# Earlier loads in the fourth chunk, inverse roots on GpSimd and a new order of steps in an adaLN / long convolution / token-MLP kernel

## The chip, the cores and the metric

One core of a Trainium2 chip runs the kernel. The metric is the device time of one execution in microseconds, the median over the runs shown. All tensors are float32. Matrix products run on TensorE (PE in the profile), elementwise work on VectorE (DVE), ScalarE (ACT) and GpSimd (POOL); all DMAs of the part around the change are issued by SyncE (SP).

## What is computed

2048 tokens (S), 640 channels (D), a token MLP of width 1728 (F):

```python
mod = (_silu(c) @ w_mod).reshape(c.shape[0], 6, 1, -1)
sa, ca, ga, sb, cb, gb = (mod[:, 0], ..., mod[:, 5])
h = _layernorm(x, axis=-1) * (1 + ca) + sa                 # x = A_q
x = x + ga * _A_ref(h, A_k, A_v, A_shift_k, A_ssm_k, A_ssm_D)
h = _layernorm(x, axis=-1) * (1 + cb) + sb
x = x + gb * _B_ref(h, B_w1, B_b1, B_w2, B_b2)
```

`_A_ref` is a short causal convolution of k over 4 tokens, times v, then a causal convolution over all 2048 tokens for each channel (by Fourier transform), times h. `_B_ref` is a layer norm of its own, then a product with w1 over the token axis, a tanh GELU, and a product with w2 back to tokens.

## The kernel before

**Chunks.** The channels are worked on in five chunks of 128 (`c` from 0 to 4; "the fourth chunk" is `c == 3`). For each chunk the Fourier transform is done as matmuls with constant matrices: `step1` (line 230) is the first stage, `f2` (line 249) the second, in eight groups `g`, each with its product of the two spectra on VectorE (L60, into `p`) and a sum on GpSimd (into `y`); `i2` (line 280) and `i1` (line 302) are the two inverse stages. `gate` multiplies the result by the layer-normed input, `add_x` adds it to the residual rows `XR(j)`, and `spill` writes these to DRAM. While one chunk goes through its inverse stages, `step1` of the next chunk runs in between.

**Loads for the tail of the program.** In the fourth chunk thirteen loads are kept in a list, `later`: nine pieces of 128 x 640 of `w_mod` (`one`, into the tiles `in`, `t` and `rows`) and four pieces of `w1` (`some`, into `aux`). `next_load()` takes the next of them: ScalarE writes one column of the place (line 543), which makes it wait until the place is free, and SyncE's DMA (line 601 or 606) waits for that write. So the position of `next_load()` in ScalarE's order paces the load. Beside them SyncE copies rows of `w1` into a scratch tensor `wc` (`copy_rows`).

**The last chunk and the start of the MLP.** With `c == 4` the loop is left after `i2`, and what follows is written out by hand. The tokens lie in 16 row blocks (`j`). For each of them the last chunk's gate must be applied, then the second layer norm: `stats` (bn_stats and bn_aggr on VectorE), `root_in` (variance to standard deviation, ScalarE), `root` (its reciprocal, corrected by one Newton step, VectorE, `newton`), `norm1` (ScalarE), `times` and `plus` (scale and shift by the modulation, VectorE; `mean` in between corrects a sum on ScalarE). The factor of h in w1's product is again normed: `square` (ScalarE) gives the variance of the scaled rows, a second root follows, then `half` (ScalarE, writes the high part of the operand) and `rest` (VectorE, the low part). All float32 operands of the MLP are split into a high and a low part, and a product is three matmul pairs: high x high, high x low, low x high (`mm`, line 465). `products` does those of the first four blocks of 128 of F, `blk[0]` to `blk[3]`, for a pair of row blocks; the weights' parts are written by `split_rows` and `split_third` (high on ScalarE, L442 and L435; low on VectorE, L60).

**What sets the order.** Each engine works through its instructions in program order; semaphores tie them. The order of this part is a list of words, which a loop runs through: `st 2 3` calls `stats(2)` and `stats(3)`, and so on (`q` root_in, `R` root, `n` norm1, `t` times, `m` mean, `p` plus, `s` square, `h` half, `r` rest, `Q` products of a pair, `v`/`wl` low parts and `vh`/`wh` high parts of the weights, `gr`/`gm`/`ga` gate and add of the rest, `gb` one row of the modulation). The table `roots` says which variances a root handles together: before, root n takes the second variances of one pair of row blocks and the first ones of the pair behind it:

```python
roots = (((), (0, 1)), ((0, 1), (2, 3)), ((2, 3), (4, 5)), ((4, 5), (6, 7)), ((6, 7), (8, 9, 10, 11)),
         ((8, 9), (12, 13)), ((10, 11), (14, 15)), ((12, 13), ()), ((14, 15), ()))
```

`warm(t, n)` (line 853) issues n matmuls whose result nobody reads, between the last inverse stages and ahead of the first products.

## Time and profile before

| | |
|---|---|
| median of 3 runs | 668.79 us (664.34 to 676.61) |
| the profiled execution's own time | 667.48 us |
| its span, first to last instruction | 665.6 us, 20814 instructions |
| mean granted TensorE clock | 0.984 |
| busy share of ACT, DVE, POOL | 47%, 75%, 21% |
| HBM read, written | 79.63 MB, 19.14 MB |

The profile is one execution. A row of a timeline has start and duration in us, engine, line of the kernel, operation, out<-in, and in brackets the idle time ahead of it with what ended it. A row of the chain of waits has start, duration and what the program's end waited for in that time; "issue" there is time in which the engine waited for nothing that the profile shows. PE is the matmul itself, PEld the load of its weights, SPq the issue of a DMA by SyncE. "PEclk" is the clock that TensorE was granted, 1.00 being full speed.

### The profile page before, as it was taken

Reading aid. Unit: us, or ns where it says so; the run is one execution under the profiler, and the core shown is the slowest. Engines: PE = TensorE matmul, PEld = TensorE weight load, DVE = VectorE, ACT = ScalarE, POOL = GpSimd, SP = SyncE. Lnnn points to the kernel's source line nnn. Section 1 sums busy time; section 2 is a strip of 40 time slices with the busy share of each in tenths; the row PEclk is TensorE's granted clock in tenths of the full one; section 3 lists DMA queues with packets and bytes.
Section 4 is the critical chain, followed back from the end, with each engine's and each line's share of the span. In section 5 each row is a group of like instructions: output and inputs, shape, how many; then the busy total and the mean of one; then the engine's idle time right before and its main releaser. Section 6 shows DMA issues by size and latency. Waiting matters only on the chain.

```text
span 665.6 us, 20814 instructions
## 1 busy us (share of the span) xinstructions
PE 618.9 (93%) x9089; PEld 597.4 (90%) x9089; DVE 497.0 (75%) x844; ACT 311.0 (47%) x497; POOL 138.3 (21%) x138
## 2 busy tenths in 40 slices
PE   0599878899999989999999999999999999999997
PEld 0699458799999979799999999999999999999997
DVE  7788559988888847789974214756688888888886
ACT  0574365555736637667874304343342332333331
POOL 5284017684865027000000000000000000000000
PEclk9999679999999989999999999999999999999999
DMA  9967997818642645514008530975698555345601
GB/s 183 215 200 209 383 177 154 187 41 193 129 77 67 196 125 154 182 33 96 1 1 156 97 64 1 218 210 145 191 354 264 173 180 159 101 143 170 189 32 39
DMA packets 175568, 98.01 MB, mean 147 GB/s; under 512 B 89939, under 2 KB 165494, under 8 KB 175222
## 3 DMA queue, kind: packets, MB, share of 16 engines
q1 hardware_dynamic: 170930, 95.38, 54.4%
q10 hardware_dynamic: 4548, 1.31, 1.1%
q8 instruction: 71, 1.16, 0.7%
q14 instruction: 19, 0.16, 0.1%
HBM read 79.63 MB, written 19.14 MB: 148 GB/s over the span
## 4 chain that ended last, share of the span: by engine, by line
PE 82%; DVE 9%; DMA 3%; issue 2%; ACT 2%; SPq 1%; ACTq 0%; DVEq 0%
PE pst L1173 26%; PE pst L465 23%; PE pst L230 11%; PE pst L249 9%; PE pst L280 5%; PE pst L1038 4%; PE pst L302 2%; DVE tap L60 2%; DMA aux<-in_w_mod_dram 2%; DVE kt L60 1%; DVE p L60 1%; DVE aux L60 1%; PE tap L366 1%; PE pst L377 1%; DMA in<-in_A_v_dram 1%
## 5 line engine op out<-in xcount | busy, mean ns | idle before, releaser
L249 PEld LDWEIGHTS pst<-z,w 128*64 128x64 f32 x2560 | 76.0, 138 | 9.0 <-issue 5.7
L249 PE MATMUL pst<-z,w 128*64 128x64 f32 x2560 | 77.5, 222 | 6.9 <-DVE p L60 4.4
L230 PE MATMUL pst<-v,x 128*64 128x128 f32 x640 | 45.1, 299 | 23.9 <-DVE x L60 23.3
L230 PEld LDWEIGHTS pst<-v,x 128*64 128x64 f32 x640 | 43.0, 221 | 24.6 <-issue 24.1
L235 ACT ACTIVATE z<-pst 128x1024 f32<-128x1024 f32 (+2 forms) x45 | 41.4, 932 | 46.0 <-PE pst L230 25.6
L60 DVE TENSOR_TENSOR p<-pst,kt 128x512 f32<-128x512 f32 x80 | 51.0, 683 | 14.7 <-ACT kt L255 13.3
L60 POOL TENSOR_TENSOR y<-p 128x256 f32<-128x256 f32 x72 | 54.2, 776 | 35.1 <-DVE p L60 34.7
L280 PEld LDWEIGHTS pst<-v,y 32*128 32x128 f32 x1280 | 39.0, 192 | 3.0 <-issue 1.6
L280 PE MATMUL pst<-v,y 32*128 32x64 f32 x1280 | 40.5, 277 | 0.6 <-ACT z L235 0.6
L230 PE MATMUL pst<-v,p 128*64 128x128 f32 x640 | 38.8, 280 | 1.9 <-issue 1.8
L230 PEld LDWEIGHTS pst<-v,p 128*64 128x64 f32 x640 | 36.5, 140 | 2.7 <-issue 2.2
L255 ACT ACTIVATE kt<-pst 128x512 f32<-128x512 f32 x40 | 24.0, 599 | 31.1 <-PE pst L249 13.0
L1173 PE MATMUL pst<-r_z,m_w 128*128 128x320 f32 x198 | 37.2, 309 | 0.0
L60 POOL TENSOR_TENSOR t<-in,t 128x512 f32<-128x512 f32 x20 | 30.3, 1524 | 18.1 <-DMA in<-in_A_k_dram 17.1
L60 DVE TENSOR_TENSOR tap<-tap,kt 128x512 f32<-128x512 f32 x45 | 31.4, 697 | 1.3
L60 DVE TENSOR_TENSOR kt<-in,tap 128x512 f32<-128x512 f32 x45 | 30.8, 685 | 1.4
L1173 PEld LDWEIGHTS pst<-r_z,m_w 128*128 128x128 f32 x198 | 31.1, 188 | 0.0
L288 ACT ACTIVATE z<-pst 128x512 f32<-128x512 f32 x38 | 21.6, 664 | 18.7 <-PE pst L280 18.7
L1110 ACT ACTIVATE m_w<-m_v 128x896 fp32r<-128x896 f32 x19 | 17.9, 948 | 26.3 <-DVE m_v L60 14.7
L302 PEld LDWEIGHTS pst<-z,v 64*64 64x64 f32 x1280 | 22.2, 144 | 7.9 <-issue 4.3
L302 PE MATMUL pst<-z,v 64*64 64x64 f32 x1280 | 24.1, 229 | 4.0 <-issue 2.9
L60 DVE TENSOR_TENSOR aux<-aux,g 128x1024 f32<-128x1024 f32 (+1 forms) x14 | 26.3, 1885 | 0.2
(309 smaller groups left out, 1446.6 us busy)
## 6 DMA issues: line engine op xcount, KB each, us to landing
x<-in_B_w_dram SPq DMA_DIRECT2D x18, 512.0 KB
m_v<-in_B_w_dram SPq DMA_DIRECT2D x20, 384.0 KB
aux<-in_A_ssm_k_dram SPq DMA_DIRECT2D x10, 512.0 KB
out_dram<-m_w SPq DMA_DIRECT2D x32, 160.0 KB
in<-in_A_k_dram SPq DMA_DIRECT2D x36, 128.0 KB
in<-in_A_v_dram SPq DMA_DIRECT2D x36, 128.0 KB
ts<-m_p SPq DMA_DIRECT2D x10, 320.0 KB
m_w<-xs SPq DMA_DIRECT2D x20, 160.0 KB
```

The lines of the kernel that those rows point to most:

```text
L60: TT = lambda eng, o, a, b, op: eng.tensor_tensor(o, a, b, op=op)
L230: pe.matmul(ps.rearrange("p (b m a) -> p b a m", b=2, a=4)[64 * ri:64 * ri + 64, a // 4, a % 4], lhs, F1[:, 128 * ri:128 * ri + 128], star ...
L235: act.activation(Z[:, side, t, :, k0:k1], ps.rearrange("p (b k a) -> p b k a", b=4, a=4)[:, :, k0:k1], AF.Copy)
L249: pe.matmul(pk[64 * h:64 * h + 64, kk // 4, ri, kk % 4], W2[k1 // 32][:, 2 * (k1 % 32) + ri], rhs, start=True, stop=True)
L255: act.activation(halves_(kt), pv[:, :, 1], AF.Copy)
L280: pe.matmul(pp[qd // 2][:, o:o + 64], Y[p, ri, i:i + 2].rearrange("p i k -> p (i k)"), V2[p, 64 * ri:64 * ri + 64], start=ri == 0, stop=ri ...
L288: act.activation(o, i, AF.Copy)
L302: pe.matmul(ps[64 * b:64 * b + 64, 512 * e + 64 * jj:512 * e + 64 * jj + 64], V1[p, ri, n2], T2[p, :, 32 * ri + n2], start=ri == 0, stop=r ...
L465: pe.matmul(ps[0:m, h, 0:320], w_.bitcast(F32R), r_[:, 320 * h:320 * h + 320].bitcast(F32R), start=first and i == 0, stop=last and i == 2)
L1038: pe.matmul(ps[n][:, h, 0:320], sets[n][:, j].bitcast(F32R), r[:, 320 * h:320 * h + 320].bitcast(F32R), start=j == 0 and r is hh, stop=j = ...
L1110: act.activation(W[n][0].bitcast(F32R), A[p, w_], AF.Copy)
L1173: pe.matmul(bank[n], w[:, i].bitcast(F32R), r.bitcast(F32R), start=m == 0 and k == 0, stop=m == 6 and k == 2)
```

## The change

Three things change.

First, the fourth chunk's loads: the list starts two transform groups earlier (`g == 3`), the pieces of `in` come first, one load is taken in each of groups 3 to 6 and two in group 7, and those behind `i2` are gathered (two at once) instead of spread to the first half of `i1`.

Second, the roots. The table has five roots of first variances alone and, behind them, eight of second variances alone. Root 0 stays on VectorE as it was. The others do only the reciprocal on VectorE; the Newton step, as one multiplication each by `r` and by the variance, an addition of 1.5 and a last multiplication, runs on GpSimd, with the sum of variance and epsilon taken ahead of it.

Third, the order of the last chunk. Filler matmuls go from 8 + 8 + 40 to 30; parts of the weights are split earlier; and the list of words is new, with the products taken a row block at a time: `A j` is what needs the high part, `B j` what needs the low part.

```diff
-            if cn == NC - 1 and g == 5:
+            if cn == NC - 1 and g == 3:
...
-                later.extend(one(kk, j) for kk, j in ((2, 2), (2, 0), (2, 1)) + tuple((n // 3, n % 3) for n in range(6)))
+                later.extend(one(kk, j) for kk, j in ((0, 0), (0, 1), (0, 2), (2, 2), (2, 0), (2, 1), (1, 0), (1, 1), (1, 2)))
...
-            if cn == NC - 1 and g in (6, 7):
-                next_load()
+            if cn == NC - 1 and g > 2:
+                next_load(2 if g == 7 else 1)
...
             if cn == NC - 1:
-                next_load()
+                next_load(2)
             step1(0, 2)
-            i2(1, then=next_load if cn == NC - 1 else None)
+            i2(1)
             step1(0, 3)
-            if cn == NC - 1:
-                next_load()
...
-    roots = (((), (0, 1)), ((0, 1), (2, 3)), ((2, 3), (4, 5)), ((4, 5), (6, 7)), ((6, 7), (8, 9, 10, 11)),
-             ((8, 9), (12, 13)), ((10, 11), (14, 15)), ((12, 13), ()), ((14, 15), ()))
+    roots = tuple(((), f) for f in ((0, 1), (2, 3, 4), (5, 6, 7), (8, 9, 10, 11), (12, 13, 14, 15))) + tuple(
+        ((j, j + 1), ()) for j in range(0, 16, 2))
...
     def root(n):
         o, first_ = slice(start[n], start[n + 1]), roots[n][1]
-        newton(R_[:, o], T_[:, o], TAB[:, o, 1])
+        f, m = slice(first_[0], first_[-1] + 1) if first_ else None, TAB[:, o, 0]
+        if n == 0:
+            newton(R_[:, o], T_[:, o], TAB[:, o, 1])
+            dve.scalar_tensor_tensor(nm1[:, f], m, -1.0, R_[:, o], op0=ALU.mult, op1=ALU.mult)
+            return
+        r, t, v = R_[:, o], T_[:, o], TAB[:, o, 1]
+        pool.tensor_scalar(v, v, EPS, -0.5, op0=ALU.add, op1=ALU.mult)
         if first_:
...
+            pool.tensor_scalar(m, m, -1.0, None, op0=ALU.mult)
+        dve.reciprocal(r, t)
+        TT(pool, t, r, r, ALU.mult)
+        TT(pool, t, t, v, ALU.mult)
+        pool.tensor_scalar(t, t, 1.5, None, op0=ALU.add)
+        TT(pool, r, t, r, ALU.mult)
+        if first_:
+            TT(pool, nm1[:, f], m, r, ALU.mult)
...
+    split_rows(0, X, (2,), True, False)
     ps0 = i1(0, jjs=range(2))
...
-    warm(ps1, 8)
+    mod_sum(tap, T_t[:, 0:640])
     gate(NC - 1, ps0, 0, dve, 0, 2)
...
-    warm(ps1, 8)
...
-    warm(acc[0].rearrange("p h m -> p (h m)"), 40)
+    warm(acc[0].rearrange("p h m -> p (h m)"), 30)
...
-            t 0 1 m 0 v 0 p 0 1 s 0 1 st 2 3 q 1 gr 0 gb 0 R 1 h 0 1 n 2 3
-            gm 0 t 2 3 m 1 st 4 r 0 p 2 3 s 2 3 st 5 r 1 Q 0 q 2 R 2 n 4 5 h 2 3
...
+            st 3 n 0 st 4 n 1 st 2 t 0 wh 2 t 1 u 0 wh 3 p 0 u 1 gb 0 p 1 s 0 gr 0 s 1 q 5 st 7 q 1 wh 1 R 5 1
+            wh 0 st 5 gm 0 h 1 0 ga 0 n 3 A 0 r 0 n 2 t 3 n 4 t 2 A 1 st 6 m 1 p 2 q 2 R 2 s 2 p 3 B 0 t 4 s 3
+            st 10 q 6 n 5 R 6 r 1 n 6 t 5 B 1 h 2 st 9 m 2 A 2 r 2 n 7 p 4 h 3 p 5 s 4 A 3 r 3 s 5 st 8 q 7 v 1
...
```

Here `u` is `mean` for a single row block, `A` and `B` are the two halves of a row block's products.

SyncE's queue in the fourth chunk, behind the third chunk's last copy into `wc` (lines with a minus stand in the kernel before, with a plus in the changed one; the number behind x counts DMAs in a row):

```order
 L428 DMA wc<-in_B_w_dram 64x4x512
+L601 DMA in<-in_w_mod_dram 128x640 x3
 L601 DMA rows<-in_w_mod_dram 128x640
 L428 DMA wc<-in_B_w_dram 64x4x128 x4
 L601 DMA t<-in_w_mod_dram 128x640 x2
-L601 DMA in<-in_w_mod_dram 128x640 x6
+L601 DMA in<-in_w_mod_dram 128x640 x3
 L606 DMA aux<-in_B_w_dram 64x2x512 x4
```

Three of the six loads into `in` now stand ahead of `rows` and the copies; the other loads keep their order.

TensorE from the last product with `sil` on (tap), in the kernel before: the inverse stage (L302), filler (L853), rows of the modulation spread to all partitions (L377), and the first products (L465).

```order
L366 MATMUL tap<-z,sm 32x320 x6
L302 MATMUL pst_4327<-z,v 64x64 x16
L853 MATMUL pst_4344<-wb_4130,wb_4000 128x320 x8
L302 MATMUL pst_4327<-z,v 64x64 x24
L377 MATMUL pst_4394<-t,sm 128x320 x2
L853 MATMUL pst_4344<-wb_4130,wb_4000 128x320 x8
L377 MATMUL pst_4408<-t,sm 128x320 x2
L302 MATMUL pst_4327<-z,v 64x64 x24
L302 MATMUL pst_4344<-z,v 64x64 x64
L377 MATMUL pst_4501<-t,sm 128x320 x2
L853 MATMUL pst_4504<-wb_4130,wb_4000 128x320 x40
L465 MATMUL pst_4504<-r_z,wb_4000 128x320 x4
```

The same place in the changed kernel:

```order
L366 MATMUL tap<-z,sm 32x320 x6
L302 MATMUL pst_4328<-z,v 64x64 x40
L377 MATMUL pst_4379<-t,sm 128x320 x2
L377 MATMUL pst_4387<-t,sm 128x320 x2
L302 MATMUL pst_4328<-z,v 64x64 x24
L302 MATMUL pst_4345<-z,v 64x64 x64
L377 MATMUL pst_4485<-t,sm 128x320 x2
L852 MATMUL pst_4488<-wb_4130,wb_4000 128x320 x30
L465 MATMUL pst_4488<-r_z,wb_4000 128x320 x4
```

Both groups of eight filler matmuls are gone, and ten of the last forty.

VectorE behind the gate and add of the rest of the first half (`gr`), in the kernel before (L552 and L786 statistics, L803 to L806 and L799 a root, L813 times, L834 rest):

```order
L60 TENSOR_TENSOR xa<-xa,aux 128x3x128
L803 RECIPROCAL kt<-kt 128x4
L804 SCALAR_TENSOR_TENSOR kt<-kt 128x4
L805 SCALAR_TENSOR_TENSOR kt<-kt 128x4
L806 SCALAR_TENSOR_TENSOR kt<-kt 128x4
L799 SCALAR_TENSOR_TENSOR sm<-kt 128x2
L60 TENSOR_TENSOR aux<-pst_4344,aux 128x2x512
L813 SCALAR_TENSOR_TENSOR t,sm<-t,kt 128x640 x2
```

The same place in the changed kernel (the lines have moved by six: L780 statistics, L799 a root's reciprocal, L819 times, L840 rest):

```order
L60 TENSOR_TENSOR xa<-xa,aux 128x3x128
L552 BN_STATS sm<-xa 128x6
L780 BN_AGGR kt<-sm 128x2
L799 RECIPROCAL kt<-kt 128x2
L799 RECIPROCAL kt<-kt 128x3
L552 BN_STATS sm<-xa 128x6
L780 BN_AGGR kt<-sm 128x2
L60 TENSOR_TENSOR aux<-pst_4345,aux 128x2x512
L60 TENSOR_TENSOR xb<-xb,aux 128x8x128
L840 SCALAR_TENSOR_TENSOR r_z<-t_g,kt,r_z 128x640
L819 SCALAR_TENSOR_TENSOR t,sm<-t,kt 128x640 x2
```

Of a root's five operations only the reciprocal is left on VectorE; roots 5 (of row blocks 0 and 1, second) and 1 (2 to 4, first) follow each other. On GpSimd, which had nothing to do there, these two roots are:

```order
L796 TENSOR_SCALAR kt<-kt 128x2
L60 TENSOR_TENSOR kt<-kt 128x2 x2
L802 TENSOR_SCALAR kt<-kt 128x2
L60 TENSOR_TENSOR kt<-kt 128x2
L796 TENSOR_SCALAR kt<-kt 128x3
L798 TENSOR_SCALAR kt<-kt 128x3
L60 TENSOR_TENSOR kt<-kt 128x3 x2
L802 TENSOR_SCALAR kt<-kt 128x3
L60 TENSOR_TENSOR kt<-kt 128x3
L60 TENSOR_TENSOR sm<-kt 128x3
```

Each but the first of a root waits for the one ahead of it or for the reciprocal.

More of the change, by code (lines that the diff above doesn't have):

```diff
@@ L732, in mixer_kernel @@
             load_ks(c + 2)
-        if cn == NC - 1:
-            next_load()
         for half in range(2):
@@ L834, in rest, with products @@
         dve.scalar_tensor_tensor(H[j][1].bitcast(F32R), row(j), at(2, j), H[j][0], op0=ALU.mult, op1=ALU.subtract)
-    def products(pr, fs=range(4)):
-        for f_ in fs:
+    def products(j, rest):
+        for f_ in range(4):
             if f_ == len(acc):
                 acc.append(psum().rearrange("p (h m) -> p h m", h=2))
-        js = [(f_, j) for j in (2 * pr, 2 * pr + 1) for f_ in fs]
-        if pr == 7:
-            for f_, j in sorted(js):
-                mm(acc[f_], blk[f_][0][:, j], blk[f_][1][:, j], *H[j], False, j == 15)
-            return
-        for rest in range(2):
-            for f_, j in js:
-                wh, wl = blk[f_][0][:, j], blk[f_][1][:, j]
-                mm(acc[f_], wh, wl, *H[j], j == 0 and not rest, False, ((wh, H[j][1]),) if rest else
-                   ((wh, H[j][0]), (wl, H[j][0])))
+            wh, wl = blk[f_][0][:, j], blk[f_][1][:, j]
+            mm(acc[f_], wh, wl, *H[j], j == 0 and not rest, False,
+               ((wh, H[j][1]),) if rest else ((wh, H[j][0]), (wl, H[j][0])))
     def warm(t, n):
@@ L898, in rest_of_half @@
         spill(NC - 1, (0,))
-    step = {"st": stats, "q": root_in, "R": root, "n": norm1, "t": times, "m": mean, "p": plus, "s": square,
-            "h": half, "r": rest, "Q": products, "gb": lambda _: gb(), "gm": lambda _: gate(NC - 1, ps, 1, None),
-            "ga": lambda _: gated(), "gr": lambda _: rest_of_half(), "v": last_block, "vh": lambda _: split_third(2, True, False),
+    step = {"st": stats, "q": root_in, "R": root, "n": norm1, "t": times, "m": mean, "u": lambda j: mean(j, 1),
+            "p": plus, "s": square, "h": half, "r": rest, "A": lambda j: products(j, False),
+            "B": lambda j: products(j, True), "gb": lambda _: gb(), "gm": lambda _: gate(NC - 1, ps, 1, None),
+            "ga": lambda _: gated(), "gr": lambda _: rest_of_half(), "v": last_block,
@@ L920, in mixer_kernel @@
     act.activation(su[:, 0:1], epsc, AF.Gelu_apprx_tanh)
-    products(7)
+    for f_ in range(4):
+        for j in (14, 15):
+            mm(acc[f_], blk[f_][0][:, j], blk[f_][1][:, j], *H[j], False, j == 15)
     U, full = {}, {}
```

37 lines of the change are left out of this document (15 added, 22 removed).

## The prediction

> **What bounds the kernel now.** I read the page first, then the chain of waits in order of time, then the stretches where that chain is not TensorE at full pace.
>
> ```profile
> PE 618.9 (93%) x9089; PEld 597.4 (90%) x9089; DVE 497.0 (75%) x844; ACT 311.0 (47%) x497; POOL 138.3 (21%) x138
> ...
> q8 instruction: 71, 1.16, 0.7%
> ```
>
> TensorE is busy 93% of the span, so an edit pays only where it closes a hole on TensorE or takes filler out of its queue. The second row comes back below: 71 packets, 1.16 MB, so 16 KB each; TensorE's 2 x 9089 instructions divided by 71 give 256 for each packet.
>
> The chain of waits holds such a hole in the fourth chunk. The same steps of the third chunk are the measure for it (start, us, what; pst L230 is the transform's first stage, L302 the last inverse stage).
>
> ```profile
> 186.46 2.20 PE pst L230 x31
> ...
> 195.25 5.42 PE pst L230 x96
> ...
> 230.28 1.96 PE pst L230 x26
> ...
> 234.99 2.56 issue
> 237.55 0.34 PE pst L302 x6
> 237.89 3.30 PE pst L230 x32
> ...
> 243.41 5.42 PE pst L230 x96
> ```
>
> From the fourth block of L230 to the group of 96 the third chunk takes 195.25 - 186.46 = 8.79 us, the fourth 243.41 - 230.28 = 13.13 us: 4.34 us more for the same matmuls. Of these, 2.56 us are a stop with no waiting instruction behind it ("issue"), and the next block of 32 takes 3.30 us where a third of 5.42 us is 1.81 us. Windows (width; busy time and count of TensorE, its weight loads, VectorE, ScalarE, GpSimd; granted clock, DMA share, GB/s) and the queue of SyncE show what surrounds it.
>
> ```profile
> 235.00:236.00 1.00, 0.00 (x0) 0.00 (x0) 0.00 (x0) 0.00 (x0) 0.00 (x0) 1.00 0.38 100
> ...
> 238.00:239.00 1.00, 1.00 (x14) 1.00 (x14) 1.00 (x1) 0.00 (x0) 0.00 (x0) 0.60 1.01 295
> ...
> 240.00:241.00 1.00, 1.00 (x12) 0.79 (x8) 0.00 (x0) 0.00 (x0) 1.00 (x1) 0.50 0.00 0
> ...
> 210.00:215.00 5.00, 5.00 (x178) 5.00 (x176) 3.43 (x6) 3.49 (x9) 3.94 (x7) 1.00 0.01 3
> ...
> 221.13 10.61 SPq L601 DMA_DIRECT2D in<-in_w_mod_dram x6
> 232.52 4.42 SPq L606 DMA_DIRECT2D aux<-in_B_w_dram x4
> ```
>
> At 235 every engine is idle, not TensorE alone; the DMA engines are at 0.4 and then at their full share with the ten loads that SyncE issues from 221 to 237, and after the stop the clock is granted at 0.5 to 0.6. TensorE stops with six matmuls of a stage left, which no data could hold. I read it as TensorE waiting for its next 16 KB of instructions, whose packet stands behind the loads. Ten microseconds earlier the DMA engines are empty (0.01).
>
> The second stretch is the start of the token MLP, where TensorE first runs filler (L853) and then the products (L465).
>
> ```profile
> 288.77 6.13 PE L853 MATMUL pst<-wb,wb 128*128 128x320 f32 x40
> 294.74 7.22 PE L465 MATMUL pst<-r_z,wb 128*128 128x320 f32 x48
> ...
> 309.81 14.45 PE pst L465 x96
> ...
> 352.58 2.80 PE L465 MATMUL pst<-r_z,wb0b 128*128 128x320 f32 x18
> ```
>
> The products of 16 row blocks are 384 matmuls. 96 of them are done by 309.81, where the chain goes over to TensorE for good, and the other 288 by 352.58: 0.1485 us each, with no hole. Everything later follows on TensorE, so what the end of these products gains, the span gains.
>
> **The change, part by part.**
>
> *The loads.* They are the same loads and the same bytes. Ahead, SyncE gets three of them, then `rows` and the four copies into `wc`, released one by one by ScalarE from the transform's fourth group on, so about 209 instead of 219 us, in the stretch where the DMA engines are idle; nothing else stands in SyncE's queue there that waits for them. The last four, released at 232 to 235 before, go out behind the first inverse stage, near 226. Traffic should be over before the last inverse stage starts at 233. ScalarE pays one short instruction a group (one column) in time that it has spare. If the stop goes and with it the low clock, the term is between 2.56 + (3.30 - 1.81) = 4.05 us and 4.34 us less; if only the stop shrinks, nothing to 2.5. I take -3.9.
>
> [...]
>
> *The products' start.* Rows for the prices, VectorE first (start, duration), then ScalarE and GpSimd:
>
> ```profile
> 278.77 0.42 DVE L60 TENSOR_TENSOR aux<-pst,aux 128x256 f32<-128x256 f32 x1 [0.90 <-PE pst L302]
> 279.24 0.43 DVE L60 TENSOR_TENSOR xa<-xa,aux 128x256 f32<-128x256 f32 x1
> ...
> 283.85 0.82 DVE L813 SCALAR_TENSOR_TENSOR t_g<-t_g,kt 128x640 f32<-128x640 f32 x1 [0.96 <-ACT t_g L809]
> ...
> 285.41 0.69 DVE L60 TENSOR_TENSOR wb<-x,wb 128x512 fp32r<-128x512 f32 x1
> 286.27 1.68 DVE L821 SCALAR_TENSOR_TENSOR t_g<-t_g,sm,kt 128x640 f32<-128x640 f32 x2 [0.17 <-ACT sm L817]
> 287.87 0.29 DVE L552 BATCH_NORM_STATS2 sm<-xa 128x6 f32<-128x128 f32 x1
> ...
> 288.40 0.24 DVE L552 BATCH_NORM_STATS2 sm<-xa 128x6 f32<-128x128 f32 x1
> ...
> 288.88 0.50 DVE L60 TENSOR_TENSOR aux<-pst,aux 128x384 f32<-128x384 f32 x1
> ...
> 289.88 0.17 DVE L803 RECIPROCAL kt<-kt 128x4 f32<-128x4 f32 x1
> ...
> 290.76 1.22 DVE L60 TENSOR_TENSOR aux<-pst,aux 128x1024 f32<-128x1024 f32 x1
> ...
> 298.03 0.82 DVE L834 SCALAR_TENSOR_TENSOR r_z<-t_g,kt,r_z 128x640 fp32r<-128x640 f32 x1
> ...
> 290.68 1.55 ACT L831 ACTIVATE r_z<-t_g,kt 128x640 fp32r<-128x640 f32 x2 [0.57 <-DVE kt L806]
> ...
> L351 POOL TENSOR_SCALAR sm<-sm 128x16 f32<-128x16 f32 x1 | 0.3, 261 | 15.6 <-ACT sm L350 15.6
> ...
> L60 POOL TENSOR_TENSOR aux<-aux,rows 1x64 f32<-1x64 f32 x10 | 3.5, 354 | 19.6 <-DMA aux<-in_A_ssm_k_dram 14.6 <-issue 4.8
> ...
> 133.67 1.29 POOL L60 TENSOR_TENSOR t<-t 128x512 f32<-128x512 f32 x1
> 135.03 1.29 POOL L60 TENSOR_TENSOR t<-in,t 128x512 f32<-128x512 f32 x1
> ...
> 136.40 3.20 POOL L60 TENSOR_TENSOR t<-t 128x512 f32<-128x512 f32 x1
> ```
>
> From start to start: statistics of a row block 0.53, "times" 0.78, "plus" 0.80, "rest" 0.78, a low part 0.69, gate and add of two blocks 0.93, of three 289.88 - 288.88 = 1.00, of eight 1.22 each, a root with its five VectorE operations 290.76 - 289.88 = 0.88, each fifth 0.18. On ScalarE half() takes 0.74.
>
> A root on GpSimd: the trace has no operation on 2 to 4 columns there. The nearest are 0.261 us (16 columns) and 0.354 us (64 elements on one partition); from one dependent operation to the next 1.36 us pass at 1.29 us of duration, so 0.07 more. One step is thus 0.33 to 0.42 us; I take 0.33, since 16 columns lie nearer. If the fixed part shrinks further with the columns, 0.25 is the lower end.
>
> The path to the products of row block 1, "B 1", where TensorE is held longest: VectorE, from its first gate at 278.77 up to "r 1", has 9 statistics (4.77), 5 times (3.90), 4 plus (3.20), 1 low part (0.69), 2 rests (1.56), the gates and adds (0.93 + 2 x 1.00 + 2.44 = 5.37), root 0 (0.88) and 4 reciprocals at 0.18 to 0.20 (0.80): 21.2 us, to 299.9. The first reciprocal ends at about 289.8; root 5 and root 1 then stand in GpSimd's queue in a row, 11 steps, 3.6 us, and the next "times" on VectorE needs root 1's mean and a 0.9 us ScalarE operation: 0.6 us of waiting. With 0.3 us of handing over, "B 1" starts near 300.9. "A 0" needs root 5 (4 steps, 1.3 us) and two halves (1.5 us): 292.8. So TensorE starts the products about 2 us earlier than at 294.74, does A 0, A 1 and B 0 (40 matmuls, 5.9 us, to 298.7) and waits 2.2 us. From 300.9 on, 344 matmuls take 51.1 us, to 352.0: -0.6 against 352.58. The 26 filler matmuls that go (some 3.9 us) therefore yield little: VectorE's queue, not TensorE's, sets "B 1".
>
> Later VectorE is relieved: of nine roots at 0.7 to 0.9 us, 7.6 us in all, one stays, and twelve reciprocals (2.4) come: about 4.3 us freed over 50 us, while TensorE asks 3.56 us for a row block and VectorE 2.9 (0.53 + 0.78 + 0.80 + 0.78). The seven low parts (4.8 us) are there as before. So nothing is late behind "B 1" as long as a GpSimd step stays near 0.33. At 0.42, 11 steps put "B 1" 1.0 us back and a root each some tenths: tail +2. At 0.25 VectorE alone sets it: -1.1.
>
> Sum on the profiled execution's 667.48 us: -3.9 - 0.6 = -4.5, so 663.0. It lies 1.3 us below the median of the runs shown, 668.79, whose two nearest differ by 4.4 us, so I add nothing. What measurement can tell from no change is 2%: under 655.4 or over 682.2.
>
> **Rivals.**
>
> *The stop stays* (chance 0.2). It may not come from the loads: they run from 221 on, and TensorE stops only at 235. Then only the tail counts: 666.9. Against it: the six matmuls left over, and the DMA share of 1.01 right behind.
>
> *GpSimd's roots become the wait* (0.13), the one that ends slower. The row at 136.40 is the same operation as the ones ahead of it, but takes 3.20 instead of 1.29 us; VectorE ran operations there with two inputs in SBUF, and "times", "plus" and "rest" are of that kind. If a small step stretches by the same 2.5, it takes 0.26 x 2.5 + 0.07 = 0.72. Twelve roots with 52 chained steps (8 of four, 4 of five) grow by 0.39 each: up to 20 us with nothing hidden, so 683. From 0.42 on each further 0.01 costs about 0.5 us, so the loads' gain is used up, and the kernel slower than before, from about 0.46 on. For it: the wait is in every pair's path and ScalarE's queue stands behind it ("h", then the next "n"). Against it: a step moves 2 to 4 elements, and the 1.9 us lost at 136.40 are spread over 512 of them.
>
> [...]
>
> *The clock falls in the new holes* (0.15). TensorE gets holes of some 1.5 us before "A 0" and 2.2 before "B 1".
>
> ```profile
> 87.71 2.30 PE L377 MATMUL pst<-kt,sm 1*128 1x320 f32 x12 [1.61 <-ACT kt L370]
> ...
> 88.00:90.00 2.00, 2.00 (x12) 0.82 (x8) 0.00 (x0) 1.18 (x5) 0.00 (x0) 0.50 0.39 48
> ...
> 99.67 1.58 PE L230 MATMUL pst<-v,p 128*64 128x128 f32 x25 [1.84 <-issue]
> ...
> 100.00:102.00 2.00, 2.00 (x41) 2.00 (x39) 2.00 (x2) 0.99 (x1) 1.92 (x2) 1.00 0.86 195
> ```
>
> A hole of 1.61 us was followed by half the clock, one of 1.84 was not. Half the clock for about 3.3 us (as from 238 to 241) costs 1.7 us; behind "A 0" the next hole takes it up, behind "B 1" it counts: 664.7.
>
> **How the numbers follow.** Forecast 663.0 (0.5), stop stays 666.9 (0.2), clock 664.7 (0.15), GpSimd 668 to 683 and beyond (0.13), the rest unnamed. The forecast's own range is 662 to 667 by the bounds (-4.3 - 1.1; -2.5 + 2). Runs of one kernel lie some 2 us to either side, which gives 658 as the low end; 673 takes in the first two rivals and the milder part of the third. All but the strongest form of the third stays within 2%: faster 0.03, same 0.89, slower 0.08.
>
> **What would show it.** In the changed trace: SyncE's loads end before 230; no "issue" piece in the fourth chunk's last inverse stage, and its 13.13 us go down to about 9; "A 0" near 293 and "B 1" near 301; GpSimd steps 0.3 to 0.35 us apart; the products end near 348, 4.5 us earlier in absolute time. It is wrong if a stop turns up elsewhere between 205 and 245, if GpSimd steps lie over 0.42 us apart, or if the products wait for ScalarE or GpSimd after "B 1".

## The result, and the profile after

The changed kernel is slower, by less than the 2% that count as a change: 669.66 us median of 20 runs (666.01 to 677.39) against 666.09 us of the kernel before in 20 runs (662.58 to 676.61). The ratio is 1.0067, with a 95% interval of 1.0046 to 1.0088; the executions that the record lists as slow (of the changed kernel those of 676.66 and 677.39 us) are left out of it, so it is not the ratio of the two medians. The profiled execution took 672.81 us (span 671.0).

The page's rows on the engines and on the chain's shares, of the kernel after:

```profile
PE 613.1 (91%) x9063; PEld 592.9 (88%) x9063; DVE 494.1 (74%) x818; ACT 312.6 (47%) x502; POOL 163.7 (24%) x206
PE 68%; DVE 9%; SPq 7%; DMA 6%; POOL 4%; issue 3%; ACT 2%; ACTq 0%; DVEq 0%; POOLq 0%
```

TensorE is busy 5.8 us less than before, and GpSimd has 68 operations and 25.4 us more. POOL has become 4% of the chain.

The fourth chunk in the chain of waits, after; the first row, from the rows of TensorE, is the start of the chunk's second transform stage (`f2`, L249):

```profile
204.05 15.15 PE L249 MATMUL pst<-z,w 128*64 128x64 f32 x512 [0.44 <-ACT z L235]
...
235.51 2.08 PE pst L302 x122
237.58 0.77 issue
238.69 1.90 PE pst L230 x32
240.59 2.30 PE pst L302 x128
242.89 5.42 PE pst L230 x96
```

The stop of 2.56 us is one of 0.77 us, and the block of 32 behind it takes 1.90 us instead of 3.30. The same start in the kernel before, and the first matmul of the stage behind the first products in both kernels (before, then after):

```profile
201.08 15.15 PE L249 MATMUL pst<-z,w 128*64 128x64 f32 x512 [0.44 <-ACT z L235]
```

```profile
380.90 23.53 PE pst L1038 x160
```

```profile
385.79 23.53 PE pst L1038 x160
```

From there, 201.08, to the group of 96 at 243.41 the kernel before took 42.33 us, after it is 242.89 - 204.05 = 38.84: 3.5 us less. From the group of 96 to L1038 it was 137.49 us, and now it is 385.79 - 242.89 = 142.90: 5.4 us more. (That the chunk starts 3 us later, in code that is the same, is scatter between executions: over all traces the stage starts between 199.9 and 206.5 us.) So the loss lies in the token MLP's start. TensorE there, after, from the filler (L852) through the products (L465); in brackets the wait ahead of a group and who ended it:

```profile
286.42 4.66 PE L852 MATMUL pst<-wb,wb 128*128 128x320 f32 x30
292.06 6.15 PE L465 MATMUL pst<-r_z,wb 128*128 128x320 f32 x40 [0.97 <-ACT r_z L837]
300.68 1.44 PE L465 MATMUL pst<-r_z,wb 128*128 128x320 f32 x8 [2.47 <-DVE r_z L840]
304.05 4.64 PE L465 MATMUL pst<-r_z,wb 128*128 128x320 f32 x16 [1.94 <-ACT r_z L837]
308.49 3.18 PE L465 MATMUL pst<-r_v,wb 128*128 128x320 f32 x16
...
343.30 14.34 PE L465 MATMUL pst<-h_x,wb 128*128 128x320 f32 x96 [0.73 <-ACT h_x L837]
```

"A 0" starts at 292.06 and "B 1" at 300.68, within 0.8 us of the forecast's 292.8 and 300.9. Behind "B 1" two more holes follow, and the groups at 304.05 and 308.49 take 4.64 and 3.18 us for 16 matmuls, which took 2.52 us in the kernel before at 304.78 with the clock at 1.00. The windows give the clock (seventh number):

```profile
302.00:304.00 2.00, 0.12 (x1) 0.00 (x0) 1.33 (x4) 1.87 (x4) 0.97 (x3) 0.79 0.00 0
304.00:306.00 2.00, 1.95 (x7) 1.95 (x8) 1.97 (x3) 1.97 (x4) 0.00 (x0) 0.50 0.00 0
```

The chain of waits names what comes before the last hole. After, ahead of the last four row blocks:

```profile
340.42 0.88 POOL kt L60
341.37 0.74 POOL kt L802
342.42 0.84 ACT h_x L837
343.30 42.49 PE pst L465 x288
```

GpSimd's corrections of the last root, then "h", then TensorE without a wait to the end of the products. Before, TensorE had the chain from 309.81 on; now it gets it at 343.30.

### The profile page after: what moved, and what is told of

It reads as the page before. It is cut to its first block, busy times and chain, and to the rows that moved or that the text cites. A ratio compares the mean times of both kernels' runs of the same rounds, so it can differ in the third digit from the quotient of the medians.

```text
span 671.0 us, 20808 instructions
## 1 busy us (share of the span) xinstructions
PE 613.1 (91%) x9063; PEld 592.9 (88%) x9063; DVE 494.1 (74%) x818; ACT 312.6 (47%) x502; POOL 163.7 (24%) x206
## 3 DMA queue, kind: packets, MB, share of 16 engines
q8 instruction: 71, 1.16, 0.8%
## 4 chain that ended last, share of the span: by engine, by line
PE 68%; DVE 9%; SPq 7%; DMA 6%; POOL 4%; issue 3%; ACT 2%; ACTq 0%; DVEq 0%; POOLq 0%
PE pst L1173 25%; PE pst L465 18%; PE pst L249 7%; PE pst L230 7%; PE pst L280 5%; PE pst L1038 4%; SPq L534 3%; PE pst L302 3%; DMA in<-in_A_k_dram 2%; DVE tap L60 2%; POOL kt L60 2%; DMA aux<-in_w_mod_dram 2%; SPq L167 2%; DVE kt L60 1%; SPq L145 1%
## 5 line engine op out<-in xcount | busy, mean ns | idle before, releaser
L249 PE MATMUL pst<-z,w 128*64 128x64 f32 x2560 | 77.6, 222 | 9.0 <-DVE p L60 5.5
L249 PEld LDWEIGHTS pst<-z,w 128*64 128x64 f32 x2560 | 76.0, 138 | 11.1 <-issue 7.8
L230 PE MATMUL pst<-v,p 128*64 128x128 f32 x640 | 36.7, 274 | 2.0 <-ACT p L177 1.4
L230 PEld LDWEIGHTS pst<-v,p 128*64 128x64 f32 x640 | 35.0, 137 | 2.5 <-ACT p L177 1.6
L465 PE MATMUL pst<-r_z,wb 128*128 128x320 f32 x144 | 24.6, 330 | 5.4 <-ACT r_z L837 2.9
L302 PEld LDWEIGHTS pst<-z,v 64*64 64x64 f32 x1280 | 21.9, 140 | 8.1 <-issue 3.7
L465 PEld LDWEIGHTS pst<-r_z,wb 128*128 128x128 f32 x144 | 23.2, 203 | 6.4 <-ACT r_z L837 3.7
```

The lines of the kernel that those rows point to most:

```text
L230: pe.matmul(ps.rearrange("p (b m a) -> p b a m", b=2, a=4)[64 * ri:64 * ri + 64, a // 4, a % 4], lhs, F1[:, 128 * ri:128 * ri + 128], star ...
L249: pe.matmul(pk[64 * h:64 * h + 64, kk // 4, ri, kk % 4], W2[k1 // 32][:, 2 * (k1 % 32) + ri], rhs, start=True, stop=True)
L302: pe.matmul(ps[64 * b:64 * b + 64, 512 * e + 64 * jj:512 * e + 64 * jj + 64], V1[p, ri, n2], T2[p, :, 32 * ri + n2], start=ri == 0, stop=r ...
L465: pe.matmul(ps[0:m, h, 0:320], w_.bitcast(F32R), r_[:, 320 * h:320 * h + 320].bitcast(F32R), start=first and i == 0, stop=last and i == 2)
```

## The experiments

Three theories on the token MLP's start: that GpSimd's small steps are held up by VectorE and make the roots late (1), that the new order makes "B 1" late whoever corrects the roots (2), and that the half clock behind the holes is the loss (3). One number is compared over all kernels, "filler to L1038": from the start of the last group of filler matmuls to the first matmul of the stage behind the products, both from the kernel's own trace. It leaves out the loads and the scatter ahead of it. Ratios are to the kernel before, run beside it on the same chip.

| kernel | order | roots corrected on | filler to L1038, us | ratio (95% interval) |
|---|---|---|---|---|
| before | old | VectorE | 92.13 | 1 |
| loads alone | old | VectorE | 92.13 | 0.9977 (0.9956 to 0.9998) |
| loads, 28 fillers | old | VectorE | 91.79 | 0.9999 (0.9970 to 1.0029) |
| loads, no correction | old | none | 90.76 | 0.9974 (0.9946 to 1.0002) |
| loads, no correction, 28 fillers | old | none | 90.19 | 0.9948 (0.9917 to 0.9979) |
| old order, GpSimd (old loads) | old | GpSimd | 101.24 | 1.0170 (1.0120 to 1.0219) |
| after | new | GpSimd | 99.37 | 1.0067 (1.0046 to 1.0088) |
| old loads | new | GpSimd | 99.37 | 1.0103 (1.0068 to 1.0139) |
| roots on VectorE | new | VectorE | 96.28 | 1.0053 (1.0025 to 1.0081) |
| no correction | new | none | 92.10 | 0.9946 (0.9908 to 0.9984) |
| second roots on VectorE | new | both | 96.52 | 1.0013 (0.9985 to 1.0041) |

The fillers start 1 to 2 us earlier, counted from the group of 96, in the new order (43.5 us behind it after, 45.4 before), which the fourth column leaves out.

### The parts apart

Loads alone is the kernel before with these and the other lines on the loads:

```diff
-            if cn == NC - 1 and g == 5:
+            if cn == NC - 1 and g == 3:
...
-            if cn == NC - 1 and g in (6, 7):
-                next_load()
+            if cn == NC - 1 and g > 2:
+                next_load(2 if g == 7 else 1)
```

> The kernel before with the loads' part of the change alone. Theory L: the stop of 2.56 us comes from the loads; the stretch from the second inverse stage to the third chunk-high group shrinks from 42.3 to about 38.8 us as in the changed kernel, so 3.5 us less than before, ratio 0.995. Rival (the traces differ by scatter, the stop stays or moves): within 1 us of before, ratio 1.000, with a stop of 2 us or more somewhere between 205 and 245.

Old loads is the changed kernel with the same lines turned back:

> The changed kernel with the loads as before, so roots and order alone. If the two parts add up, the tail's loss of 5.4 us stands alone: ratio 1.008 (1.007 to 1.012), and with it the holes of 2 to 2.5 us before the second low part of the products and behind it, at half clock. Rival (the loss comes from the loads, which make something else late): ratio 1.000.

Measured: 0.9977, a gain of 1.5 us (0.1 to 2.9), halfway between theory and rival, and 1.0103. The two parts add up: without the loads' part the changed kernel is 0.36% or 2.4 us slower still (the two intervals overlap), and filler to L1038 is the same to 0.01 us with the old loads and the new, 92.13 twice and 99.37 twice. So the loads are a gain, though not of 3.5 us, and the whole loss lies in roots and order. The chain of the changed kernel with the old loads shows on what one trace misled:

```profile
234.63 0.98 issue
235.96 1.90 PE pst L230 x32
237.85 1.54 PE pst L302 x90
239.39 1.05 issue
240.44 0.81 PE pst L302 x38
```

With the same loads as before there are two stops here, of 0.98 and 1.05 us, and no half clock. The first stop lies six matmuls ahead of the end of its group, as before and after, the second 6 + 32 + 90 = 128 matmuls, so 256 instructions of TensorE (a matmul and its weight load each), behind it. The changed kernel's page has 71 packets and 1.16 MB of instructions too (q8) and 2 x 9063 instructions of TensorE, so 255 for each packet of 16 KB: by the author's estimate the stops sit where such a block begins. How long they are differs from one execution to the next. In sum the stops of this stage are 2.03 us here, 2.56 before and 3.05 in the third profile with the old loads (old order, GpSimd: 2.00 and 1.05). So 2.56 us was a fair size; but the low clock behind it, with 3.30 us for the block of 32 that takes 1.90 here, is in the trace of before alone.

From the second transform stage to the group of 96 the three profiles with the old loads took 42.3, 40.1 and 41.8 us, the 13 with the new ones 37.6 to 39.8, on the mean 38.9: 2.5 us less. The stops do not go with the new loads: 0 to 1.5 us are left in this stage. And some of these profiles have stops further on, of up to 2.74 us, on the mean 0.7 us, which the three with the old loads do not have. One of them, in the changed kernel with fillers (below):

```profile
256.22 0.33 issue
256.55 3.94 PE pst L249 x127
260.49 2.63 issue
```

The places are 127 matmuls apart by the trace, near the 128 above. 2.5 - 0.7 = 1.8 us lies between the 1.5 and 2.4 measured.

### Who corrects the roots

Roots on VectorE: the changed kernel, with the correction put back.

```diff
-        r, t, v = R_[:, o], T_[:, o], TAB[:, o, 1]
-        pool.tensor_scalar(v, v, EPS, -0.5, op0=ALU.add, op1=ALU.mult)
...
+        newton(R_[:, o], T_[:, o], TAB[:, o, 1])
```

> The changed kernel, loads and order as they are, with every root corrected on VectorE again as before. Theory 1 (GpSimd's small steps are held by VectorE's operations with two SBUF inputs): the waits behind the roots go and the tail is back to that of before, some 5 us under the changed kernel, ratio to before 0.995. Theory 2 (the new order itself makes the second row block's products late, whoever does the roots, since VectorE's queue sets them): the roots' 0.7 us each come back into VectorE's queue and the holes stay, 2.5 to 5 us in all, ratio about 1.006, as the changed kernel.

Old order, GpSimd: the kernel before, its table of roots and its steps, with the changed kernel's corrections on GpSimd in `root`.

> The kernel before, with its order and its loads, whose roots (but the first) are corrected on GpSimd. Theory 1: each root stands directly ahead of its use there, so eight roots of 6 to 7 held steps (0.45 us each on the mean) lie in the path: 5 to 9 us more than before, ratio 1.008 to 1.013, with steps of 0.6 us and more beside VectorE's 640-column operations. If small steps keep to some 0.28 us: not over 3 us more, ratio up to 1.004.

No correction: the changed kernel with `dve.reciprocal` alone in `root`, and the `nm1` operation on VectorE. It leaves out the Newton step of all roots but the first, so it serves to measure and not as a replacement.

> The changed kernel without the correction of the roots behind the first (left out: the Newton step; the reciprocal of the square root is used as it is, and the negative mean times root is one VectorE operation), so without the 68 GpSimd steps. Theory 1 (waiting for GpSimd's held steps makes most of the tail's loss): the holes ahead of row block 1's low products and of row block 2 shrink to 1.5 us and less in sum, the clock stays up, 4 to 6 us under the changed kernel, ratio to before 0.998 to 1.001. Theory 2 (VectorE's queue in the new order sets row block 1): that hole stays at 2 us or more with half the clock behind it, only the second hole goes: ratio 1.003 to 1.004.

Second roots on VectorE: the roots of table entries 5 to 12 go back, the four first ones stay, and with them 28 of the 68 GpSimd steps.

```diff
+        if n > 4:
+            newton(R_[:, o], T_[:, o], TAB[:, o, 1])
+            return
```

> The changed kernel with the eight second roots of two row blocks corrected on VectorE, and only the four first ones on GpSimd, 24 steps instead of 68. If the held steps between square and half make the loss: from the first filler to the next stage about 95 us (99.4 in the changed kernel, 96.3 with all on VectorE), ratio 1.000 to 1.002, better than either. If the first roots are what is late: 97 us and more, 1.006.

Measured: 1.0053, 1.0170, 0.9946 and 1.0013. The first alone speaks for theory 2, which said 1.006 where theory 1 said 0.995: with the correction on VectorE the new order still loses. But without any correction it is as fast from the fillers on as the kernel before (92.10), so theory 2 falls as a cause by itself: the order is not late, it has no room for what a root costs. Against that kernel it loses 4.2 us with the correction on VectorE and 7.3 us with the one on GpSimd. The old order takes GpSimd's corrections worse still (9.1 us; 1.0170 where 1.008 to 1.013 was expected), which fits that each root stands right ahead of its use there. The second roots back on VectorE bring 2.9 of the 7.3 us (96.52), by this number as much as all of them back (96.28). TensorE's first hole ahead of "B 1", with the roots on VectorE and then without a correction:

```profile
300.59 5.32 PE L465 MATMUL pst<-r_z,wb 128*128 128x320 f32 x24 [3.70 <-DVE r_z L832]
```

```profile
296.46 3.99 PE L465 MATMUL pst<-r_z,wb 128*128 128x320 f32 x24 [1.44 <-DVE r_z L832]
```

VectorE's roots cost the new order 4.2 us and the old one 1.4 (92.13 against 90.76, both with the new loads and 40 fillers). A count agrees with this, though no run tests it as the reason: the new table has 13 roots, the old one 9, and a root costs the same four or five short operations for two columns as for six (in the trace of before 0.15 to 0.16 us each on two columns at 281.49, 0.17 to 0.19 in the root of six at 313.91).

### The half clock

Fillers: the changed kernel with matmuls of 192 columns in the two holes behind "B 0" and "B 1", written to columns that nothing reads.

```diff
-... p 3 B 0 t 4 s 3
+... p 3 B 0 F 24 t 4 s 3
-... t 5 B 1 h 2 ...
+... t 5 B 1 F 20 h 2 ...
```

> The changed kernel with filler matmuls of 192 columns (into columns of the accumulators that nothing reads) in TensorE's queue: 24 behind the row block 0's low products, 20 behind those of row block 1, some 2.2 and 1.8 us, so a little less than the holes of 2.47 and 1.94 us there. Theory 3 (the holes make the clock fall, and half the clock from 302 to 310 us costs 2.8 us): the clock stays at 1.00 and the products end 2.8 us sooner, ratio to before 1.0025, to the changed kernel 0.996. Rival (the clock falls for another reason, or data come no sooner): no change, ratio to before 1.0067.

The same with the roots on VectorE (36 and 1 fillers):

> The changed kernel with its roots corrected on VectorE (ratio to before 1.0053, hole of 3.70 us ahead of row block 1's low products, half the clock for 4 us behind it), with 36 filler matmuls of 192 columns, some 3.2 us, in that hole. Theory 3: the clock stays full, 1.8 us less, ratio to before 1.0026. What is then left over the kernel with the loads' part alone (0.9977), some 3 us, is the order's own: row block 1's low products come that much too late. Rival: the clock falls all the same, 1.005.

Measured: 1.0075 (1.0036 to 1.0113), and 1.0000 (0.9963 to 1.0037), where 1.0025 and 1.0026 were expected. The first is no gain over 1.0067. The second is lower than the 1.0053 without fillers, by more than the theory gives, but the intervals overlap and the medians of the kernel itself are the same (667.62 us with, 667.82 without); it is the kernel before beside it that differs. The traces decide: the clock did stay at 1.00 in every window from 296 to 314 us, and yet filler to L1038 is 99.10 and 96.30 us, against 99.37 and 96.28. TensorE in the kernel with fillers shows where the gain went:

```profile
302.50 1.36 PE L465 MATMUL pst<-r_z,wb 128*128 128x320 f32 x8
...
305.90 2.53 PE L465 MATMUL pst<-r_z,wb 128*128 128x320 f32 x16
...
320.78 7.33 PE L465 MATMUL pst<-h_a,wb 128*128 128x320 f32 x48 [0.58 <-ACT h_a L837]
329.09 3.80 PE L465 MATMUL pst<-h_a,wb 128*128 128x320 f32 x24 [0.98 <-ACT h_a L837]
...
344.51 14.33 PE L465 MATMUL pst<-h_x,wb 128*128 128x320 f32 x96 [0.74 <-ACT h_x L837]
```

Full speed at 305.90 (2.53 us for 16), and two new holes at 320 and 329, for "h" that comes when it came before. The early holes and the half clock only took up slack: the end is set by the roots of the last row blocks. Theory 3 falls here. It was then tried where nothing late follows, in the kernel with the second roots on VectorE, whose TensorE rows are

```profile
299.66 1.44 PE L465 MATMUL pst<-r_z,wb 128*128 128x320 f32 x8 [2.09 <-DVE r_z L843]
302.20 4.63 PE L465 MATMUL pst<-r_z,wb 128*128 128x320 f32 x16 [1.10 <-ACT r_z L840]
306.63 3.17 PE L465 MATMUL pst<-r_v,wb 128*128 128x320 f32 x16
```

with no hole behind them, and whose clock is 0.50 in the windows from 302 to 308 us. It got 19 fillers behind "B 0" and 9 behind "B 1":

> The changed kernel with its second roots corrected on VectorE (ratio 1.0013; no hole is left behind row block 2, and half the clock from 301.6 to 308 us costs 3.0 us on 32 matmuls), with 19 and 9 filler matmuls of 192 columns in the two holes ahead of row blocks 1 and 2. Theory (half the clock costs time only where TensorE waits for nothing later, so nothing in the changed kernel, but 3 us here): from the first filler to the next stage 93.5 us instead of 96.5, ratio 0.997 to 0.998, as the loads' part alone. Rival (the clock is of no account here either, a later wait takes the gain): 96 us, ratio 1.001.

Measured: 0.9964 (0.9937 to 0.9991), where the same kernel without the fillers had 1.0013 (0.9985 to 1.0041), so the intervals just overlap. Filler to L1038 is 95.33 us against 96.52, nearer to the rival's 96 than to 93.5, since a later hole of 0.73 us opens; the clock is 1.00 in every window from 296 to 310 us. So the half clock costs something there: 1.2 us by the traces, 2.4 by the medians (664.40 against 666.79 us). This kernel keeps the whole computation and its ratio is the lowest of those that do. Loads alone (0.9977) cannot be told from it, though, and its tail is longer than that of the old order (95.33 against 92.13), so that the traces do not say why it should be the faster one.

### What holds a GpSimd step

The steps of the changed kernel between 280 and 345 us, in groups (mean ns of one behind the comma), two kinds of step:

```profile
L60 POOL TENSOR_TENSOR kt<-kt 128x2 f32<-128x2 f32 x21 | 7.8, 371 | 1.8
L802 POOL TENSOR_SCALAR kt<-kt 128x3 f32<-128x3 f32 x2 | 1.7, 828 | 0.2
```

and single steps beside VectorE's operations in order of time:

```profile
299.75 0.87 DVE L840 SCALAR_TENSOR_TENSOR r_z<-t_g,kt,r_z 128x640 fp32r<-128x640 f32 x1
299.80 0.91 POOL L802 TENSOR_SCALAR kt<-kt 128x3 f32<-128x3 f32 x1
300.80 0.20 POOL L60 TENSOR_TENSOR kt<-kt 128x3 f32<-128x3 f32 x1
...
302.26 0.82 DVE L819 SCALAR_TENSOR_TENSOR xa<-xa,kt 128x640 f32<-128x640 f32 x1 [1.64 <-ACT xa L815]
302.49 0.65 POOL L60 TENSOR_TENSOR kt<-kt 128x2 f32<-128x2 f32 x1
```

The step at 299.80 ends at 300.71, VectorE's operation at 300.62; the one at 302.49 ends at 303.14, VectorE's at 303.08. The step at 300.80, with VectorE idle, takes 0.20 us. Over all 68 steps of the trace: 38 that meet no VectorE operation with two inputs in SBUF take 0.20 us on the mean (0.25 at most), 18 of them beside other operations of VectorE; the 30 that meet one take 0.645 us, up to 1.57, and end some 0.06 us behind such an operation (median). To see whether the end of the operation releases the step, two of VectorE's three kinds of such operations on 640 columns ("plus", shown here, and "rest" likewise; not "times") were cut in halves:

```diff
-        dve.scalar_tensor_tensor(t, t, su[:, j:j + 1], SB, op0=ALU.add, op1=ALU.add)
+        for o in (slice(0, 320), slice(320, 640)):
+            dve.scalar_tensor_tensor(t[:, o], t[:, o], su[:, j:j + 1], SB[:, o], op0=ALU.add, op1=ALU.add)
...
```

> The changed kernel with two of VectorE's long operations with two inputs in SBUF (the ones that add the mean and shift, and that make the low part) cut into two halves of 320 columns each. Theory 1 (a small GpSimd step that starts beside such an operation ends when that operation ends): steps held by these two kinds last 0.45 us and less, only those beside the uncut product stay near 0.8; the mean of the two-column steps falls from 350 ns to 250 to 300. Rival (steps are slow for a reason of their own, their number of inputs or the time from one to the next): the mean stays at 350 ns. The time is of no account here, since VectorE gets 28 instructions more of some 0.1 us each.

Measured in one execution: the steps beside the halves do end with the halves.

```profile
300.35 0.53 DVE L828 SCALAR_TENSOR_TENSOR t<-t,sm,kt 128x320 f32<-128x320 f32 x1
300.46 0.51 POOL L798 TENSOR_SCALAR kt<-kt 128x3 f32<-128x3 f32 x1
```

The step ends at 300.97, the half at 300.88. But the mean of the two-column steps stayed at 366 ns (371 above), where 250 to 300 was expected, which is a miss: the held steps got shorter, but more steps met such an operation (39 of 68, at 0.505 us each; 30 at 0.645 before the cut). The release is shown, the cure is not.

The other direction came with the low parts of the weights' last rows, moved from VectorE to GpSimd in the kernel with the roots on VectorE:

```diff
-            "wl": lambda f: split_rows(3, P, (f,), False, True)}
+            "wl": lambda f: split_rows(3, P, (f,), False, True, pool)}
```

> The changed kernel with the roots corrected on VectorE, and the four low parts of the weights' last rows, which nothing needs before the last four row blocks, on GpSimd instead of VectorE. Theory (with its roots back, VectorE's queue sets the new order's end: 54.6 of 60 us busy): 2.4 us leave VectorE, and the time from the first filler to the next stage goes from 96.3 to about 94 us, ratio to before 1.002. Rival (operations on GpSimd and VectorE with two inputs in SBUF shut each other out): the low parts take 2 to 4 us each, VectorE is held in turn, no gain or slower, 1.005 and more.

Measured: 1.0070 (1.0039 to 1.0100), so the rival: no gain over 1.0053. Filler to L1038 is 97.41 us (96.28 without the move; some 1 us of it may be the fillers' own, whose 30 matmuls took 7.12 us in this execution and 4.67 without the move), where 94 was expected.

```profile
324.03 2.55 POOL L60 TENSOR_TENSOR wb<-p,wb 128x512 fp32r<-128x512 f32 x2 [35.23 <-ACT kt L785]
324.07 1.27 DVE L802 SCALAR_TENSOR_TENSOR kt<-kt 128x2 f32<-128x2 f32 x1
325.37 1.22 DVE L803 SCALAR_TENSOR_TENSOR kt<-kt 128x2 f32<-128x2 f32 x1
326.63 0.16 DVE L804 SCALAR_TENSOR_TENSOR kt<-kt 128x2 f32<-128x2 f32 x1
```

Two steps of a root on VectorE take 1.27 and 1.22 us instead of 0.16, each as long as the GpSimd operation beside it. In all these rows the one that comes first goes ahead, and the other ends only with it or just behind it, however small its own is (0.65 us for a step that takes 0.20 alone, 1.27 for 0.16).

### What the old order could give

The loads' part with the old order, first without the correction and with 40 fillers, then with 28, then with the correction and 28:

```diff
-    warm(acc[0].rearrange("p h m -> p (h m)"), 40)
+    warm(acc[0].rearrange("p h m -> p (h m)"), 28)
```

> The loads' part with the order of before, without the correction of the roots (left out: the Newton step on VectorE; the reciprocal of the square root is used as it is). TensorE has only 0.5 us of holes there from its 40 filler matmuls on, so theory: roots that cost nothing gain at most that, ratio to before 0.997, as the loads' part alone (0.9977). If VectorE sets the end there too: 2 us or more under that, 0.994.

> The same (order of before, loads' part, correction of the roots left out) with 28 filler matmuls instead of 40, so 1.8 us less in TensorE's queue. Theory: with free roots the old order can start that much earlier, and gets what the new order gets without the correction (0.9946): ratio 0.994 to 0.996, so the new order has no worth of its own. Rival: the old order's data come too late for that, holes take the fillers' place, ratio as with 40 fillers, 0.997, and the new order is worth some 1.5 us once roots are free.

> The loads' part with the order and the VectorE roots of before, and 28 filler matmuls instead of 40. Theory (in the order of before, with its roots on VectorE, ScalarE's and VectorE's chain to row block 2 ends just behind TensorE's fillers): the 1.8 us of fillers come back as a hole ahead of row block 2, the end stays, ratio 0.9977 as with 40. If TensorE alone sets it: 1.8 us less, ratio 0.995, and 2 us better than any kernel with its correction so far.

Measured: 0.9974, 0.9948 and 0.9999. The old order with free roots and fewer fillers gets what the new order gets with free roots (0.9946): the new order has no worth of its own that these runs show. With the correction, 12 fillers fewer give nothing, and the time comes back as a hole ahead of row block 2:

```profile
306.75 2.62 PE L465 MATMUL pst<-r_z,wb 128*128 128x320 f32 x16 [1.81 <-ACT r_z L825]
```

## Why the prediction was wrong

Forecast were 663.0 us and a gain of 4.5 us; measured is a loss of 4.5 us (0.67% of 666).

*The loads, -3.9.* Right in sign and place, too large: 1.5 to 2.4 us. The stop itself was well sized (2.56 us; 2.03 and 3.05 in the other two profiles with the old loads). The step that failed is that it goes as a whole and takes the low clock with it. The low clock was taken from one execution, and the other two do not have it; and with the new loads 0 to 1.5 us of stops stay in the stage and 0.7 us on the mean come further on. The sign "a stop elsewhere between 205 and 245" came true in part: the changed kernel's own trace has 0.77 us at the old place, six matmuls ahead of the group's end, with the DMA engines nearly idle around it (share 0.01, the last number but one below), and the changed kernel with the roots on VectorE has one of 1.18 us at 216. That two stops lie 128 matmuls, so 256 instructions, apart is measured (127 in the kernel with fillers). That TensorE waits there for a packet of instructions was the author's reading, and what would delay it, the loads alone or something else too, no run shows.

```profile
236.00:238.00 2.00, 1.58 (x106) 1.45 (x95) 0.00 (x0) 0.53 (x1) 0.00 (x0) 1.00 0.01 5
```

*"A 0" and "B 1", 292.8 and 300.9.* Right, with the hole of 2.2 us measured at 2.47. That the absolute times agree is luck in part: the forecast gives them in the time of the kernel before, without its own 3.9 us for the loads, and the changed kernel's chunk happened to start 3 us later. Counted from the group of 96, 49.4 and 57.5 us were forecast and 49.2 and 57.8 measured. VectorE's queue as counted does set a part of "B 1": without any GpSimd step it still has a hole of 1.44 us.

*VectorE relieved by 4.3 us.* About right: it is busy 57.70 us from 284 to 360 in the changed kernel, and 62.55 us with the roots on VectorE.

```profile
284.00:360.00 76.00, 69.87 (x517) 67.88 (x507) 57.70 (x118) 54.35 (x105) 26.91 (x68) 0.96 0.17 36
```

```profile
284.00:360.00 76.00, 71.32 (x477) 69.85 (x468) 62.55 (x156) 52.98 (x103) 0.00 (x0) 0.98 0.23 47
```

*"Nothing is late behind B 1 as long as a GpSimd step stays near 0.33."* This is the larger of the two steps that failed, 6 of some 8 us. A step takes 26.91 / 68 = 0.40 us and 0.08 (median) pass to the next, 0.48 together. The prediction's own price, +2 at 0.42 and 0.5 us for each 0.01 above, gives +5.0 for that; the tail lost 5.4. That the two are so close is luck in part, since the price takes every chained step to lie in the path. With the steps gone the rest of the path's sum holds: without correction, the way from the group of 96 to L1038 is 375.66 - 239.45 = 136.2 us, 1.3 less than before, where the prediction had 1.1 less for VectorE alone.

So the third rival came true in its mild form, beyond the point where it was said to decide (0.46), and its chance of 0.13 was too small. It was held down by a wrong argument: that the 1.9 us which the long GpSimd operation lost were spread over its 512 elements, so that 2 to 4 elements lose little. The wait in these traces is not per element. It lasts to the end of VectorE's operation (the step ends 0.06 us behind it, median), and a step on 2 to 4 columns that takes 0.20 us alone takes 0.65 on the mean beside one. The trace of before had this next to the row at 136.40:

```profile
136.10 2.37 DVE L60 TENSOR_TENSOR aux<-aux,g 128x2048 f32<-128x2048 f32 x1
```

VectorE's operation ends at 138.47, and the GpSimd operation begun at 136.40 ends at 139.60, 1.13 us later, where the same operation takes 1.29 in all at 133.67. Both ends of the range taken, 0.25 and 0.42, came from rows in which VectorE was not looked at. How much of the 7.3 us is the hold, and how much a chain of four or five steps would cost without it, no run separates: none has the steps without the operations that hold them.

*The clock.* The holes around "B 1" were followed by half the clock (0.50 to 0.51 in the windows from 304 to 310 us), as the clock rival said, and at a higher price: 4.64 + 3.18 us for 32 matmuls that take 2.53 + 2.52 with the clock at 1.00 (the kernel with fillers, from 305.90 on), so 2.8 us. But it cost nothing in this kernel, since the last row blocks' roots were later still, which only the fillers showed.

*The stop stays.* It did not stay as it was, nor did it go: the term is neither 0, as this rival had it, nor 3.9, but 1.5 to 2.4 us, with stops of up to 2.74 us left (the kernel with halves, at 261.59).

*Range and chances.* Within 2% was right and had 0.89. The time lies within 658 to 673; the sign of the change was wrong, because two terms went against the forecast together: 1.5 to 2.4 us on the loads, 6 us on the tail (+5.4 where -0.6 was forecast).

## What to carry to other kernels

Before short operations are moved to GpSimd, look at what VectorE runs beside them: here the 30 steps that met an operation with two inputs in SBUF took 0.645 us on the mean and the other 38 took 0.20, so such a chain of five steps is to be priced by VectorE's operations and not by its own alone. A stop seen in one profiled execution is a sample (2.56, 2.03 and 3.05 us with the same loads); its size, and what follows it, are known only from several. And closing a hole with a low clock behind it paid only where nothing later waited: filler in it showed this at once (99.10 us against 99.37 in the changed kernel, 95.33 against 96.52 with the second roots on VectorE).

## What was not expected of the hardware

Two holes of 2.47 and 1.94 us with eight matmuls between, or of 2.09 and 1.10, were followed by half the clock for some 7 us (6.8 in both by the windows), while a single one of 1.81 was not (1.00 in the windows from 306 to 310 us with 28 fillers). A single one of 1.61 was, though (the prediction's row at 87.71), so these traces give no rule by length or number. With fillers in both holes the clock stayed at 1.00 (296 to 314 us).

The hold was measured both ways: at 324.07 a VectorE operation on two columns took 1.27 us instead of 0.16, beside one of two GpSimd operations of 2.55 us together.

That the stops in TensorE's stream turn up with the DMA engines nearly idle (0.77 us at 237.58, with a DMA share of 0.01 from 236 to 238 us) is left open: no run here shows what TensorE then waits for.
